# A long-convolution and expert-routing kernel: the first step's frequencies get a DRAM tensor of their own, and the second head's loads and six pieces move behind the first products

## Chip, core and metric

The kernel runs on one core of one Trainium2 chip. The metric is the device time of one execution in microseconds. An execution is taken as the median of several runs.

## What is computed

For each of 4 sequences of 11,456 positions and 128 channels, `u = x * v` is convolved along the sequence with a filter that a small network makes from position embeddings, and the result is multiplied by `x`. Each row then goes, if a skip score is positive, through one of eight experts.

```python
h_filt = (np.maximum(pos_emb @ w1, 0.0) @ w2) * np.exp(-0.01 * pos)[:, None]
u = x * v
Uf = np.fft.rfft(u, n=2 * S, axis=1)
Hf = np.fft.rfft(h_filt, n=2 * S, axis=0)
y = x * np.fft.irfft(Uf * Hf[None, :, :], n=2 * S, axis=1)[:, :S, :]
# then: skip_score = rows @ w_skip; top-1 of 8 experts on the rows with a positive score,
# out = row + gate * relu(row @ w1[e]) @ w2[e]
```

## The kernel before, in words

The transform is done as small matrix products, in blocks of 3,840 positions (60 x 64). The 128 channels are cut into four quarters of 32, which the code calls heads (`NP = 4`, index `h`).

**First phase** (`first_phase`, `First`). Step by step, 16 steps for one head, `load` brings a 768 KB piece of x and v through SyncE's queue (L190, `wf<-xv`, three buffers), `mult` multiplies them (L197), `data` transforms the product on TensorE in two pieces (L214), ScalarE copies them out of PSUM (L216), and `store` writes 720 KB to the DRAM tensor `x1d[h]` through ScalarE's queue (L202, `x1d<-wf`, four buffers). The transform of the filter (`filt`) is woven between; GpSimd's queue stores it in 16 stores of 720 KB to `x1f` (L270).

**Second phase** (`freq_phase`). It takes four of the 60 frequencies at a time: 15 steps for one head, 60 in all; step n is called an iteration here. `load(n)` brings 256 KB of constants (L383, first head only), 768 KB of `x1d[h]` (L386) and 192 KB of `x1f` (L387), all through SyncE's queue, and three iterations ahead. `spread` makes the second transform (L400) with copies by ScalarE (L404); `join` and `mult` on VectorE multiply by the filter (L411 to L420); GpSimd adds the blocks (L493, L494); `back` transforms back on TensorE (L435), and `store` writes z (L447).

The first phase does head 0 alone. The steps of heads 1 to 3 (`others`, a generator) are done inside the second phase as pieces between its products, two pieces for a step, with the multiplication on GpSimd from step 19 on. `step` counts how many pieces are due in an iteration. In head 0 that is two, and four in some iterations. `others` multiplies one step ahead: it calls `mult(n + 1)` before `data(n)`. In the kernel before, the first three steps of head 1 (16 to 18: six pieces, `LEAD`) are done between the first loads and the first products, and the loads of their x and v are issued already in the first phase, since `ahead` looks three steps forward.

Each engine runs its instructions in the order of the program. What sets the order around the change is this order on SyncE's, ScalarE's and GpSimd's queues, and a load of `x1d[0]` waits for all 16 stores to that tensor.

Of the kernel before, what the change touches and what calls it, by code (L numbers as in the profile page):

```python
# [12 lines left out]
F32 = mybir.dt.float32  # L13
# [11 lines left out]
K1, N2 = 60, 64  # L25
L = K1 * N2
H2 = N2 // 2
NS = NB * B
N = L * NS
NP = 4  # L30
DH = D // NP
# [15 lines left out]
LEAD = 6  # L47
FLEAD = 2
FEND = 2
KS = 4  # L50
# [105 lines left out]
class First:  # L156
# [3 lines left out]
    Q = 2  # L160
# [2 lines left out]
    ALL = NP * STEPS  # L163
    XV, US, XS = 3, 2, 4

    def __init__(self, nc, i, x1d, x1f, mc, stage):
        self.nc, self.i, self.x1d, self.x1f = nc, i, x1d, x1f
        n = self.Q * self.RUN
        at = [0]

        def piece(k):
            at[0] += k * n
            return stage[:, at[0] - k * n:at[0]]
        self.xv = [piece(2).rearrange("n (a c) -> n a c", a=2) for _ in range(self.XV)]
        self.us = [piece(1) for _ in range(self.US)]
        self.xs = [piece(2)[0:2 * K1] for _ in range(self.XS)]
        self.used = at[0]
        self.c1 = mc.tile([128, 2 * K1], F32, name="c1")
        nc.sync.dma_start(self.c1, i["c1"])
        self.loaded, self.late = 0, []  # L180

    def ahead(self, step, most=XV):

        while self.loaded < min(step + most, self.ALL):
            self.load(self.loaded)
            self.loaded += 1

# [10 lines left out]

    def store(self):

        for dst, xs in self.late:
            self.nc.scalar.dma_start(dst, xs)  # L202
        self.late = []

    def data(self, step, pool):
        nc, Q, RUN = self.nc, self.Q, self.RUN
        h, ch = divmod(step, self.STEPS)
        u = self.us[step % self.US]
        xs = self.xs[step % self.XS].rearrange("k (m w) -> k m w", w=RUN)
        for q in range(Q):  # L210
            ps = [pool.tile([2 * K1, 512], F32, name="ps")[:, 0:RUN] for _ in range(2)]
            for p in range(2):
                rows = slice(p * 64, p * 64 + K1)
                nc.tensor.matmul(ps[p], self.c1[rows], u[rows, q * RUN:(q + 1) * RUN], start=True, stop=True)  # L214
            for p in range(2):
                nc.scalar.copy(xs[:, 2 * q + p], ps[p])  # L216
            if q < Q - 1:
                yield
        self.late.append((self.x1d[h][:, :, 2 * Q * ch:2 * Q * (ch + 1)].rearrange("k c m w -> (k c) m w"), xs))
        self.store()  # L220
        yield

# [69 lines left out]
def first_phase(tc, fi):  # L292

    with (
        tc.manual_schedule(),
        tc.tile_pool(name="fc", bufs=1) as fc,
        tc.tile_pool(name="fp", bufs=2) as fp,
        tc.tile_pool(name="fps", bufs=4, space=PSUM) as fps,
    ):
        f = fi.filt(fc, fp, fps)  # L300
        left = 0.0
        pieces = NB * 64 * H2 // 512 + 2 * NB * H2 // 4
        pace = (pieces - FLEAD) / (fi.Q * (fi.STEPS - FEND))
        next(f)
        fi.ahead(0, 1)
        next(f)
        fi.ahead(0)
        fi.mult(0)
        for _ in range(FLEAD):
            next(f)  # L310
        for step in range(fi.STEPS):
            for n, _ in enumerate(fi.data(step, fps)):
                if n == 0:
                    fi.ahead(step + 1)
                    if step < fi.STEPS - 1:
                        fi.mult(step + 1)
                left += pace
                while left >= 1:
                    left -= 1
                    next(f, None)  # L320
        for _ in f:
            pass


def freq_phase(tc, nc, i, fi, zd, c3, spare, loads):
# [9 lines left out]
    with (  # L335
# [9 lines left out]
        def c2(k, n=1):  # L345
            t, k = (spare, k) if k < HERE else (rest, k - HERE)
            return t[:, k * 128:(k + n) * 128]
        done = [0]

        def others():  # L350

            fi.mult(fi.STEPS)
            for n in range(fi.STEPS, fi.ALL):
                fi.mult(n + 1)
                fi.ahead(n + 1)
                for _ in fi.data(n, qps):
                    done[0] += 1
                    yield
# [18 lines left out]
        def load(n):  # L377
            h, k = divmod(n, PER)
            while done[0] < h * fi.STEPS * fi.Q:
                next(todo)  # L380
            ks = slice(KS * k, KS * k + KS)
            if h == 0:
                nc.sync.dma_start(c2(ks.start, KS), i["c2"][k])  # L383
            x1 = qx.tile([128, KS, (NS + NB) * DH], F32, name="x1")
            w = NB * DH
            nc.sync.dma_start(x1[:, :, 0:fi.RUN], fi.x1d[h][ks].rearrange("k c n w -> (c n) k w"))  # L386
            nc.sync.dma_start(x1[:, :, fi.RUN:], fi.x1f[ks, :, :, h * w:(h + 1) * w].rearrange("k c n w -> (c n) k w"))  # L387
            return x1

        def spread(n, j):  # L390
# [61 lines left out]
        todo = others()  # L452
        ys = {}
        xs = {n: load(n) for n in range(QX - 1)}
        for _ in range(LEAD):
            next(todo)
        xps, due = {}, []

        def begin(n, j):
            if n < ALL:  # L460
                spread(n, j)
        begin(0, 0)
        begin(0, 1)
        for n in range(ALL + LAG):
            back = backer(n - LAG, ys.pop(n - LAG)) if n >= LAG else lambda lo, hi: None
            if n + QX - 1 < ALL:
                xs[n + QX - 1] = load(n + QX - 1)
            if n >= ALL - PER:
                next(loads, None)

            def half(j):
                join(n, j)
                mult(y, n, j, 0)
                mult(p1, n, j, 1)
                mult(p2, n, j, 2)
                del xps[n, j]
            if n < ALL:
                y = ys[n] = qp.tile([128, NV, 2, NB, B, DH], F32, name="y", bufs=3)
                p1 = qp.tile([128, NV, 2, NB - 1, B, DH], F32, name="p1")
                p2 = qp.tile([128, NV, 2, 1, B, DH], F32, name="p2")  # L480
                half(0)
            step()
            begin(n + 1, 0)
            piece()
            back(0, 2)
            store(nc.sync if n < ALL - 4 else nc.scalar)
            if n < ALL:
                half(1)
                del xs[n]
            begin(n + 1, 1)  # L490
            if n < ALL:
                if n < ALL - 1:
                    nc.gpsimd.tensor_tensor(y[:, :, :, 1:], y[:, :, :, 1:], p1, ALU.add)  # L493
                    nc.gpsimd.tensor_tensor(y[:, :, :, 2:], y[:, :, :, 2:], p2, ALU.add)  # L494
                else:
                    nc.gpsimd.tensor_tensor(y[:, :, :, 1], y[:, :, :, 1], p1[:, :, :, 0], ALU.add)
                    nc.vector.tensor_tensor(y[:, :, :, 2], y[:, :, :, 2], p1[:, :, :, 1], ALU.add)
                    nc.vector.tensor_tensor(y[:, :, :, 2], y[:, :, :, 2], p2[:, :, :, 0], ALU.add)
            piece(ALL)
            back(2, NB)  # L500
        store(nc.scalar)


# [559 lines left out]
def out_phase(tc, i, out, zd, ex, consts):  # L1063
# [6 lines left out]
    with (  # L1070
# [3 lines left out]
      with (  # L1074
# [257 lines left out]
        for q, x in enumerate(ahead):  # L1332
            load(q, x)
# [94 lines left out]
def program(tc, i, out):  # L1428
    nc = tc.nc
    x1d = [nc.dram_tensor(f"x1d{h}", (K1, 2, N2, NS * DH), F32).ap() for h in range(NP)]  # L1430
    x1f = nc.dram_tensor("x1f", (K1, 2, N2, NB * D), F32).ap()
    zd = nc.dram_tensor("zd", (2, NP, H2 * 2 * K1 + ZR, NS * DH), F32).ap()
    lists = nc.dram_tensor("lists", (ROOM // PL, PL), I32).ap()
    with tc.tile_pool(name="mc", bufs=1) as mc:
        wf = mc.tile([128, 2 * E * F], F32, name="wf")
        fi = First(nc, i, x1d, x1f, mc, wf)
        spare = wf[:, fi.used:]
        c3 = mc.tile([128, NV, 128], F32, name="c3")
        first_phase(tc, fi)
        nc.scalar.dma_start(c3, i["c3"])  # L1440
        nc.scalar.dma_start(zd.rearrange("p h r w -> (p h) r w")[:, H2 * 2 * K1:], i["none"])
        later = {}

        def prepare():

            later["ex"] = Experts(tc, i, out, lists, mc, wf)
            yield
            later["consts"] = out_consts(nc, i, mc)
            for e in range(E):
                if e % 2 == 0:  # L1450
                    yield
                later["ex"].weights(e, 0)

            for e in range(E):
                if e != 1:
                    yield
                later["ex"].weights(e, 1)
        freq_phase(tc, nc, i, fi, zd, c3, spare, prepare())
        out_phase(tc, i, out, zd, later["ex"], later["consts"])
# [55 lines left out]
```

## Time and profile before

| | us |
|---|---|
| median of 3 runs | 1555.54 |
| lowest and highest | 1553.31, 1558.93 |
| the profiled execution | 1556.24 |
| its span, first to last instruction | 1554.5 |

The span holds the first phase up to about 125 us, the second phase up to about 690 us, and then the way back and the experts. TensorE is busy for 95% of the span, by the page.

### The profile page before, as it was taken

The numbers are of one execution on the slowest core, as the hardware profiler recorded it, in microseconds if no ns is written. First come the engines' busy times: TensorE is split into PE (matmuls) and PEld (weight loads), VectorE is DVE, ScalarE is ACT, GpSimd is POOL, SyncE is SP. The second block draws the span as 40 slices with busy tenths as digits, with TensorE's granted clock in tenths as the row PEclk, the third lists the DMA queues.
The fourth block names the chain that finished last, engine by engine and source line by source line (L and its number), as shares of the span: only waits on it lengthen the run. The fifth ranks groups of instructions, "written<-read, shape, count | busy, mean of one in ns | idle before, by whom it ended". The sixth has DMA issues, their size and how long they took to land. (4 is left out here: it accounts for less than half of the span.)

```text
span 1554.5 us, 27988 instructions
## 1 busy us (share of the span) xinstructions
PE 1477.4 (95%) x9149; PEld 902.4 (58%) x9149; DVE 1057.0 (68%) x2356; ACT 790.3 (51%) x1643; POOL 965.7 (62%) x808
## 2 busy tenths in 40 slices
PE   7994999999999999979899999999989999999997
PEld 3551344444444434434477666666667788888887
DVE  1322876777777788866876666666658877777773
ACT  4552555555555544433455454454535555556554
POOL 0100876777777766630576459528956888888765
PEclk9997999999999999989899999999999999999999
DMA  9999999999999989989877778778521111111100
GB/s 331 312 334 342 367 385 385 369 370 364 358 384 363 310 252 340 312 291 339 276 260 218 234 229 256 252 216 241 169 57 40 43 46 45 46 46 43 40 29 25
DMA packets 199289, 362.20 MB, mean 233 GB/s; under 512 B 64508, under 2 KB 138762, under 8 KB 199102
## 3 DMA queue, kind: packets, MB, share of 16 engines
q1 hardware_dynamic: 173462, 272.15, 51.9%
q10 hardware_dynamic: 10192, 52.51, 9.1%
q0 software_dynamic: 15488, 35.74, 8.4%
q8 instruction: 74, 1.21, 0.3%
q14 instruction: 73, 0.60, 0.1%
HBM read 216.89 MB, written 145.42 MB: 233 GB/s over the span
## 5 line engine op out<-in xcount | busy, mean ns | idle before, releaser
L746 POOL DMA_INDIRECT out<-o,ids x182 | 197.1, 1083 | 149.0 <-DVE o L753 112.5
L493 POOL TENSOR_TENSOR y<-y,p 128x1536 f32<-128x1536 f32 x59 | 203.6, 3450 | 98.3 <-DVE p L420 98.3
L435 PE MATMUL ps<-y,c 64*128 64x256 f32 (+1 forms) x1440 | 258.9, 490 | 3.5 <-ACT wf L216 2.7
L675 POOL DMA_INDIRECT xt<-out,ids x182 | 192.1, 1056 | 47.9 <-issue 23.5
L435 PEld LDWEIGHTS ps<-y,c 64*128 64x128 f32 x1440 | 138.6, 187 | 116.5 <-issue 83.0
L891 DVE SCALAR_TENSOR_TENSOR hh<-hp,hh 128x1024 fp32r<-128x1024 f32 (+1 forms) x124 | 150.0, 1210 | 79.2 <-ACT hh L890 79.1
L404 ACT COPY xx<-xp 128x480 f32<-128x480 f32 x240 | 112.9, 523 | 127.2 <-PE xp L400 95.1
L438 ACT COPY z<-ps 128x512 f32<-128x512 f32 x240 | 103.6, 482 | 138.3 <-PE ps L435 129.0
L890 ACT ACTIVATE hh<-hp 128x1024 fp32r<-128x1024 f32 (+1 forms) x124 | 127.6, 1029 | 90.0 <-PE hp L742 87.1
L420 DVE TENSOR_TENSOR p<-xp,xx 128x768 f32<-128x768 f32 x240 | 169.4, 748 | 0.0
L420 DVE TENSOR_TENSOR y<-xp,xx 128x1152 f32<-128x1152 f32 x120 | 162.9, 1357 | 4.1
L411 DVE TENSOR_TENSOR xx<-xp,xx 128x384 f32<-128x384 f32 x120 | 66.7, 556 | 127.0 <-ACT xx L404 127.0
L400 PE MATMUL xp<-x,wf 128*64 128x480 f32 x512 | 118.7, 586 | 21.3 <-DMA x<-x1f 17.3
L833 PEld LDWEIGHTS bank<-wd,h 128*128 128x128 f32 x896 | 104.2, 191 | 32.8 <-issue 25.9
L648 POOL MEMSET idle<- 128x512 f16 x226 | 122.4, 542 | 0.3
L216 ACT COPY wf<-ps 120x384 f32<-120x384 f32 x256 | 111.4, 501 | 21.9 <-PE ps L214 12.7
L197 POOL TENSOR_TENSOR wf<-wf 124x768 f32<-124x768 f32 x45 | 81.8, 1818 | 64.2 <-DVE xx L411 35.0
L214 PE MATMUL ps<-wf,c 60*120 60x384 f32 x512 | 118.4, 527 | 2.7 <-ACT wf L216 1.6
L626 POOL DMA_INDIRECT lists<-pl,lies x32 | 51.5, 1609 | 105.5 <-DVE step L1257 52.3
L833 PE MATMUL bank<-wd,h 128*128 128x128 f32 x896 | 114.5, 281 | 1.3 <-DVE o L753 1.3
L494 POOL TENSOR_TENSOR y<-y,p 128x768 f32<-128x768 f32 x59 | 107.2, 1817 | 4.6
L1159 PE MATMUL y<-zt,c 128*64 128x512 f32 x344 | 96.9, 632 | 10.9 <-issue 9.0
(183 smaller groups left out, 2898.7 us busy)
## 6 DMA issues: line engine op xcount, KB each, us to landing
wf<-xv SPq DMA_DIRECT2D x64, 768.0 KB
x1d<-wf ACTq DMA_DIRECT2D x64, 720.0 KB
x<-x1d SPq DMA_DIRECT2D x60, 768.0 KB
zt<-zd SPq DMA_DIRECT2D x58, 768.0 KB
zd<-z SPq DMA_DIRECT2D x108, 384.0 KB
out<-xm SPq DMA_DIRECT2D x96, 258.0 KB
ox<-xo SPq DMA_DIRECT2D x96, 256.0 KB
x1f<-fx POOLq DMA_DIRECT2D x16, 720.0 KB
```

The costliest lines, as they stand in the source:

```text
L214: nc.tensor.matmul(ps[p], self.c1[rows], u[rows, q * RUN:(q + 1) * RUN], start=True, stop=True)
L400: nc.tensor.matmul(xp[p * 64:(p + 1) * 64, c, 0:(NS + NB) * DH], c2(n % PER * KS + k)[:, c * 64:(c + 1) * 64], x1[:, k], start=True, stop= ...
L404: nc.scalar.copy(xx[:, 2 * c, 0:w], xp[:, c, 0:w])
L420: nc.vector.tensor_tensor(o[:, :, j].rearrange("p v m b d -> p v (m b) d"), v[:, :, None, s * DH:(s + 1) * DH].broadcast_to([128, NV, m, DH]),
L435: nc.tensor.matmul(zps[p], c3[r, v], yv[r, v, :, lo:hi], start=(v == 0), stop=(v == NV - 1))
L493: nc.gpsimd.tensor_tensor(y[:, :, :, 1:], y[:, :, :, 1:], p1, ALU.add)
L648: self.nc.gpsimd.memset(self.idle, 0.0)
L675: ins = nc.gpsimd.indirect_dma_start(out=xt[:, j], out_offset=None, in_=self.rows[0:have], in_offset=bass.IndirectOffsetOnAxis(ap=ids[:, j ...
L746: ins = nc.gpsimd.indirect_dma_start(out=self.rows, out_offset=bass.IndirectOffsetOnAxis(ap=ids[:, j:j + 1], axis=0), in_=o, in_offset=Non ...
L833: nc.tensor.matmul(bank[:, j * D:(j + 1) * D], h[f // nf][:, k:k + 128], wd[u][:, f * D:(f + 1) * D], start=(f == 0), stop=(f == F // 128 ...
L890: nc.scalar.activation(v[:, 0], hp, AF.Relu)
L891: nc.vector.scalar_tensor_tensor(v[:, 1], hp, 0.0, v[:, 0].bitcast(F32), ALU.max, ALU.subtract)
```

## The change

A DRAM tensor `x1s` takes the first four frequencies of head 0 (`KS = 4`). Each of the 16 stores of head 0 is cut in two: eight rows go to `x1s` through GpSimd's queue, the other 112 rows to `x1d[0]` through ScalarE's queue as before. The first iteration's loads of `x1s` and `x1f` are issued on GpSimd's queue instead of SyncE's. In the first phase `ahead` stops at the last step of head 0; the loads for steps 16 to 18 are issued when `others` first runs. The six pieces come behind `begin(0, 0)` and `begin(0, 1)`, the products of the first iteration.

```diff
     def ahead(self, step, most=XV):
-        while self.loaded < min(step + most, self.ALL):
+        while self.loaded < min(step + most, self.ALL if step >= self.STEPS else self.STEPS):
@@ data
-        self.late.append((self.x1d[h][:, :, 2 * Q * ch:2 * Q * (ch + 1)].rearrange("k c m w -> (k c) m w"), xs))
+        m = slice(2 * Q * ch, 2 * Q * (ch + 1))
+        k = KS if h == 0 else 0
+        if k:
+            self.late.append((nc.gpsimd, self.x1s[:, :, m].rearrange("k c m w -> (k c) m w"), xs[:2 * k]))
+        self.late.append((nc.scalar, self.x1d[h][k:, :, m].rearrange("k c m w -> (k c) m w"), xs[2 * k:]))
@@ first_phase
-                    fi.ahead(step + 1)
+                    fi.ahead(min(step + 1, fi.STEPS - 1))
@@ others
+            fi.ahead(fi.STEPS)
             fi.mult(fi.STEPS)
@@ load
-            nc.sync.dma_start(x1[:, :, 0:fi.RUN], fi.x1d[h][ks].rearrange("k c n w -> (c n) k w"))
-            nc.sync.dma_start(x1[:, :, fi.RUN:], fi.x1f[ks, :, :, h * w:(h + 1) * w].rearrange("k c n w -> (c n) k w"))
+            eng, src = (nc.gpsimd, fi.x1s) if n == 0 else (nc.sync, fi.x1d[h][ks])
+            eng.dma_start(x1[:, :, 0:fi.RUN], src.rearrange("k c n w -> (c n) k w"))
+            eng.dma_start(x1[:, :, fi.RUN:], fi.x1f[ks, :, :, h * w:(h + 1) * w].rearrange("k c n w -> (c n) k w"))
@@ freq_phase
-        for _ in range(LEAD):
-            next(todo)
         xps, due = {}, []
         begin(0, 0)
         begin(0, 1)
+        for _ in range(LEAD):
+            next(todo)
```

## Rows read from the trace of the kernel before

**Rows 1.** Busy time by stretch: us, each engine's busy us, clock, DMA share, GB/s.

```profile
0.00:100.00 100.00, 89.67 (x581) 47.29 (x583) 26.31 (x34) 48.36 (x98) 6.69 (x16) 1.00 0.93 323
100.00:118.00 18.00, 17.65 (x111) 8.91 (x108) 4.50 (x6) 9.68 (x21) 1.56 (x3) 1.00 0.97 338
118.00:126.00 8.00, 6.32 (x28) 3.47 (x27) 2.87 (x3) 5.47 (x15) 0.52 (x1) 1.00 0.94 373
126.00:136.00 10.00, 1.62 (x8) 0.75 (x8) 0.00 (x0) 2.29 (x6) 0.00 (x0) 0.60 0.93 322
...
150.00:175.00 25.00, 20.46 (x102) 7.94 (x102) 23.08 (x34) 11.92 (x28) 21.15 (x10) 1.00 1.04 388
175.00:180.00 5.00, 5.00 (x32) 2.15 (x28) 3.33 (x6) 2.79 (x7) 3.54 (x2) 1.00 0.94 312
180.00:206.00 26.00, 26.00 (x132) 10.79 (x132) 19.84 (x30) 14.66 (x34) 21.19 (x9) 1.00 1.02 377
206.00:253.00 47.00, 45.91 (x241) 20.72 (x242) 33.51 (x48) 25.81 (x61) 35.45 (x16) 1.00 1.03 386
```

**Rows 2.** SyncE's queue: wait (total, times, longest us), then loads (start, us).

```profile
SPq L386 <- DMA x1d<-wf: 18.3, 2, 15.4
...
132.51 0.39 SPq L386 DMA_DIRECT2D x<-x1d  x1
136.33 0.37 SPq L387 DMA_DIRECT2D x<-x1f  x1
```

**Rows 3.** Timeline of GpSimd (start us, us, what): filter store, iterations with two steps.

```profile
118.01 0.52 POOL L270 DMA_DIRECT2D x1f<-fx  x1 [0.32 <-ACT fx L264]
...
204.27 3.76 POOL L197 TENSOR_TENSOR wf<-wf 124x768 f32<-124x768 f32 x2 [0.47 <-PE ps L214]
207.99 3.43 POOL L493 TENSOR_TENSOR y<-y,p 128x1536 f32<-128x1536 f32 x1
...
255.99 1.81 POOL L197 TENSOR_TENSOR wf<-wf 124x768 f32<-124x768 f32 x1 [0.66 <-DMA wf<-xv]
```

**Rows 4.** Timeline of VectorE and TensorE: step 18's product, first products, first join.

```profile
124.88 0.96 DVE L197 TENSOR_TENSOR wf<-wf 124x768 f32<-124x768 f32 x1 [3.68 <-DMA wf<-xv]
...
144.88 5.17 PE L400 MATMUL xp<-x,wf 128*64 128x480 f32 x16 [17.27 <-DMA x<-x1f]
...
149.36 0.56 DVE L411 TENSOR_TENSOR xx<-xp,xx 128x384 f32<-128x384 f32 x1 [23.52 <-ACT xx L404]
```

**Rows 5.** DMA, 0 to 140 us: GB/s in 40 slices, then issues, KB each.

```profile
GB/s 99 316 410 413 400 214 375 341 424 381 277 191 305 309 292 317 328 346 363 367 321 302 298 248 324 369 390 320 348 303 344 349 365 335 392 355 337 335 293 303
...
wf<-xv SPq DMA_DIRECT2D x19, 768.0 KB
x1d<-wf ACTq DMA_DIRECT2D x19, 720.0 KB
x1f<-fx POOLq DMA_DIRECT2D x16, 720.0 KB
post<-post SPq DMA_DIRECT2D x12, 256.0 KB
```

**Rows 6.** Timeline of ScalarE (start us, us, what): stores of steps 13, 15; a copy.

```profile
114.15 0.32 ACTq L202 DMA_DIRECT2D x1d<-wf  x1
...
121.36 0.32 ACTq L202 DMA_DIRECT2D x1d<-wf  x1
...
125.04 1.63 ACT L216 COPY wf<-ps 120x384 f32<-120x384 f32 x4 [1.63 <-DMA x1d<-wf]
```

**Rows 7.** The page's groups: GpSimd's indirect loads, busy us and mean ns.

```profile
L675 POOL DMA_INDIRECT xt<-out,ids x182 | 192.1, 1056 | 47.9 <-issue 23.5
```

**Rows 8.** DMA, 140 to 270 us: GB/s in 40 slices of 3.25 us.

```profile
GB/s 359 217 379 411 395 375 369 383 394 380 402 287 308 415 344 329 425 394 392 382 394 393 380 406 348 357 395 364 411 406 384 398 387 376 408 411 395 393 384 296
```

**Rows 9.** One stretch as in rows 1, and TensorE's timeline in it.

```profile
255.00:260.00 5.00, 3.39 (x15) 2.29 (x16) 2.16 (x3) 2.11 (x6) 4.34 (x3) 0.76 1.03 399
...
256.88 2.97 PE L435 MATMUL ps<-y,c 64*128 64x256 f32 x12 [1.61 <-ACT wf L216]
```

More of the change, by code (lines that the diff above doesn't have):

```diff
@@ L164, with __init__ @@
     XV, US, XS = 3, 2, 4
-    def __init__(self, nc, i, x1d, x1f, mc, stage):
-        self.nc, self.i, self.x1d, self.x1f = nc, i, x1d, x1f
+    def __init__(self, nc, i, x1s, x1d, x1f, mc, stage):
+        self.nc, self.i, self.x1s, self.x1d, self.x1f = nc, i, x1s, x1d, x1f
         n = self.Q * self.RUN
@@ L199, in store @@
     def store(self):
-        for dst, xs in self.late:
-            self.nc.scalar.dma_start(dst, xs)
+        for eng, dst, xs in self.late:
+            eng.dma_start(dst, xs)
         self.late = []
@@ L1430, in program @@
     x1d = [nc.dram_tensor(f"x1d{h}", (K1, 2, N2, NS * DH), F32).ap() for h in range(NP)]
+    x1s = nc.dram_tensor("x1s", (KS, 2, N2, NS * DH), F32).ap()
     x1f = nc.dram_tensor("x1f", (K1, 2, N2, NB * D), F32).ap()
@@ L1435, in program @@
         wf = mc.tile([128, 2 * E * F], F32, name="wf")
-        fi = First(nc, i, x1d, x1f, mc, wf)
+        fi = First(nc, i, x1s, x1d, x1f, mc, wf)
         spare = wf[:, fi.used:]
```

## The prediction

> **What bounds the kernel now.** I read the table by stretch first: around the change it shows TensorE doing 1.62 us of work in the ten microseconds from 126 [rows 1]. The timelines say why. The first load of the second phase waits 15.4 us for the stores to `x1d` and goes out at 132.51; its `x1f` half goes out at 136.33 [rows 2], when the last filter store, issued at 118.01 [rows 3], has landed. The first products start at 144.88 and the first `join` at 149.36 [rows 4]. That gap is what the change can shorten.
>
> The same table has a second reading, and I think it decides. The DMA engines show a share of 0.93 to 0.97 up to 136 and of 1.02 to 1.04 at 377 to 388 GB/s from 150 to 253, but for a dip to 312 at 175 to 180 [rows 1]. So transfers, and not TensorE alone, pace head 0. Where it hurts is seen on GpSimd in the iterations with two steps: the pair of multiplications at 204.27 takes 3.76 us, 0.14 more than two of 1.81, and the second one of the pair at 255.99 waits 0.66 us for its load of x and v [rows 3]. Slack there is nil: GpSimd's block sums (L493) are queued right behind the pair, at 207.99, and TensorE's way back waits for them.
>
> **What moves ahead of the first load.** Up to 140 us 19 loads of xv, 19 stores to `x1d`, 16 to `x1f` and 12 loads of positions are issued [rows 5]: 14.94 + 14.01 + 11.80 + 3.15 = 43.9 MB, with some 1.0 MB of constants 44.9 MB. The rates add up to 32.3 + 6.1 + 3.0 + 3.2 = 44.6 MB by 136 [rows 1]: the gate at 136.33 is the moment when everything ahead has gone through. The change takes 3 x 768 KB of loads and 3 x 720 KB of stores out of that, 4.57 MB, and leaves 40.3. These bytes were through by 118 + (40.3 - 38.4) / 0.373 = 123. But step 15's stores are issued only at 121.36 [rows 6], by the engines' pace; one takes between 2.0 us (720 KB at 373 GB/s) and the 10.9 us from 114.15 to 125.04 of step 13's [rows 6]. With the queues nearly empty I take 4: the gate falls at 125.5 instead of 136.3, between 123 and 130.
>
> **The own tensor and GpSimd's queue.** Sixteen more stores at 0.52 us [rows 3] are 8.3 us on GpSimd, which is all but idle there (1.56 us of 18, 0.52 of 8) [rows 1]. The two loads cost GpSimd between 0.52 us each and, by rows handled, 8 x 1.06 = 8.4 us for both (1,024 short rows against 128 of an indirect load [rows 7]); I take the lower end, the direct transfer being nearest. The new wait on GpSimd holds up the `x1f` half, the first multiplications of `others` and the first block sums; all need later data. The load of `x1s` cannot bring the first products forward alone, because they need `x1f` too, gated 3.8 us later than `x1d` before.
>
> **First products.** From the gate to the first product it took 144.88 - 136.33 = 8.6 us: now 125.5 + 8.6 = 134, plus 5.2 for the sixteen products [rows 4], 139.3. With the high GpSimd price 142 and 147.
>
> **The six pieces.** Their loads now stand on SyncE's queue behind the loads of iterations 1 and 2, and VectorE's three multiplications (0.96 us each [rows 4]) stand ahead of the first `join`. So the join waits for step 18's load: three iterations' x1 (2.95 MB), constants 0.26 and xv 2.36, 5.6 MB, behind a start-up of about 2 us (the kernel's first 3.5 us slice moved 99 GB/s against 316 in the next [rows 5]). At 322 to 388 GB/s that is 14 to 17 us: 142 to 145, and with the last multiplication the join at 143 to 146; I take 145, at most 148 with the gate late, against 149.36. Behind those loads on SyncE wait the xv of steps 19 to 21 (each for its buffer) and the fourth iteration's loads, which so shift with the join. The engines are 4.4 us ahead here. Counted alone that is 1556.24 - 4.4 = 1551.8.
>
> **What takes it back.** The six transfers are not gone, only later, and the DMA engines stand still meanwhile. At 125.5 before had moved 41.2 MB, after 40.3: 0.9 behind. Start-up of 2 us at 345 GB/s: another 0.7. The dip at 175 to 180 gives back (388 - 312) x 5 us = 0.38 MB, since the engines now feed the queues earlier; so does the slice of 3.25 us from 143 on at 217 GB/s between 359 and 379 ([rows 8], the second slice), some 0.45 MB, a pause that comes from SyncE's short queue at that point. That leaves 0.8 MB, at 385 GB/s 2.1 us. Up to 206 both kernels need the same bytes, so the pair's second multiplication, at 206.2 before, comes at about 208: the 4.4 us become a wait of 6.5 us on GpSimd, then on TensorE. The pair at 256 meets full queues again (1.03 [rows 1]), so the delay stays. From there on all is shifted alike. The sum: 1556.24 + 2.1 = 1558.3 for the profiled execution, and 0.7 less against the median of 1555.54: **1557.6**. With the gate 2.5 us either way and start-up between 0 and 4 us: 1553.5 to 1561.
>
> In the ten microseconds from 126, when little but ScalarE's stores is under way, 322 GB/s are moved, and 388 from 150 on [rows 1]; no row shows single engines. [...]
>
> **Rivals.** (1) The start is kept, faster: the loads of the pairs are late by their place in the queue, not for want of bandwidth, and come earlier with everything else. For it: the dip at 175 to 180, and slack before the ordinary iterations. Against it: shares over 1.0 everywhere else and bytes that do not shrink. Then 1555.5 - 4.4 = 1551.1, and with the join at its earliest, 142.5, 1548.7. [...] (3) The change does not do what it says: the last `x1f` store, still in GpSimd's queue with the small stores, lands as late as before (136), because its share of the DMA engines does not grow when the other two queues fall idle. Then first products at 145, six pieces behind them, the join at some 152, 2.6 later than before, and by the pair most of that is covered by the loads: 1558.
>
> **How the numbers follow.** A measurement of this kernel can tell some 0.3% from no change, 4.7 us: below 1550.9 and above 1560.2. Forecast 0.60, of which 0.06 lies above; rival 1 0.20, of which 0.13 below 1550.9; rival 2 0.12, 0.10 above; rival 3 0.08, 0.01 above. Faster 0.13, same 0.70, slower 0.17. Range 1550.5 to 1562: it leaves out the far ends of rivals 1 and 2.
>
> **What would show it.** Right: GpSimd's loads of `x1s` and `x1f` issued at about 126, first products near 134, the first join near 145, a DMA rate well under 338 GB/s somewhere between 110 and 128, and GpSimd's first pair of multiplications in one iteration split, its second half waiting for xv until about 208. Wrong: a pair without a wait while the join is early (rival 1), or a low granted clock after both pairs with loads long there (rival 2), or loads on GpSimd at 134 or later (rival 3). The forecast falls if DMA engines in 150 to 206 move clearly more than 390 GB/s.

## The result and the profile after

| | before | after |
|---|---|---|
| median | 1556.44 (5 runs) | 1568.33 (5 runs) |
| lowest, highest | 1553.31, 1558.93 | 1561.16, 1570.41 |
| profiled execution, its span | 1556.24, 1554.5 | 1561.16, 1559.4 |

The changed kernel is slower: ratio 1.0065, 95% interval 1.0040 to 1.0089 (the two medians alone give 1.0076). The forecast was 1557.6 us, range 1550.5 to 1562. The profiled execution is the fastest of its five, so its trace shows the smaller part of the loss, 4.9 us.

The table by stretch, as in [rows 1] (us, each engine's busy us, clock, DMA share, GB/s):

```profile
0.00:100.00 100.00, 84.70 (x538) 44.09 (x540) 24.75 (x32) 46.14 (x93) 11.32 (x25) 0.97 0.91 314
100.00:118.00 18.00, 18.00 (x138) 10.29 (x136) 6.05 (x8) 9.20 (x20) 3.61 (x7) 1.00 0.89 299
118.00:126.00 8.00, 5.47 (x26) 2.64 (x22) 0.00 (x0) 5.31 (x12) 2.07 (x4) 1.00 0.88 259
126.00:136.00 10.00, 0.00 (x0) 0.00 (x0) 0.00 (x0) 0.00 (x0) 0.94 (x2) 0.62 0.61 184
...
180.00:206.00 26.00, 25.90 (x138) 11.78 (x136) 19.78 (x28) 14.20 (x34) 18.81 (x10) 1.00 1.04 398
```

Two things differ. In the first 100 us TensorE has worked 4.97 us less than before (84.70 against 89.67). And between 126 and 136 us no engine computes at all, while the DMA engines move 184 GB/s at a share of 0.61, against 322 at 0.93. They had room, and the first load waited all the same. The timeline (start us, us, what) shows for how long:

```profile
124.65 0.31 ACTq L202 DMA_DIRECT2D x1d<-wf  x1
124.91 0.52 POOL L202 DMA_DIRECT2D x1s<-wf  x1 [1.58 <-ACT wf L216]
135.06 0.81 POOL L392 DMA_DIRECT2D x<-x1s  x1 [9.63 <-DMA x1s<-wf]
135.37 0.39 SPq L392 DMA_DIRECT2D x<-x1d  x1
135.86 0.78 POOL L393 DMA_DIRECT2D x<-x1f  x1
...
143.76 5.95 PE L406 MATMUL xp<-x,wf 128*64 128x480 f32 x16 [20.27 <-DMA x<-x1f]
...
153.58 0.96 DVE L197 TENSOR_TENSOR wf<-wf 124x768 f32<-124x768 f32 x1 [0.49 <-DMA wf<-xv]
154.45 0.55 DVE L417 TENSOR_TENSOR xx<-xp,xx 128x384 f32<-128x384 f32 x1
```

Step 15's stores are issued at 124.65 and 124.91 us, against 121.36 for the one store of before [rows 6]. The load that waits for the 48 KB of `x1s` goes out 10.15 us later, at 135.06 where 125.5 was forecast, and 0.3 us before the one that waits for the 672 KB of `x1d`. The first products start at 143.76, 1.1 us ahead of [rows 4], but the first join at 154.45, 5.1 us behind it, because the products of steps 16 to 18 now stand in front of it and wait for loads issued after the gate. GpSimd's block sums begin 5.5 us later than before (162.70 against 157.20), the seventh stands 7.6 us later (215.56 against [rows 3]) and the fourteenth 7.1 us (287.75 against 280.69).

Most of that loss falls in four short stretches of the first phase, 65 to 85 us (2.8 of the 4.97 us; 36 of the 43 matmuls that TensorE is behind by at 100 us):

```profile
65.00:70.00 5.00, 1.16 (x4) 0.48 (x4) 1.12 (x2) 1.24 (x3) 0.00 (x0) 0.69 0.99 365
70.00:75.00 5.00, 5.00 (x24) 2.20 (x22) 0.00 (x0) 2.14 (x5) 0.51 (x1) 0.62 0.78 284
75.00:80.00 5.00, 5.00 (x40) 2.82 (x38) 1.46 (x3) 1.84 (x4) 0.54 (x2) 1.00 0.05 21
80.00:85.00 5.00, 5.00 (x40) 2.74 (x38) 1.48 (x2) 2.79 (x6) 1.02 (x2) 1.00 1.03 257
```

and in ScalarE's and TensorE's rows at its start (start us, us, what):

```profile
68.76 0.59 ACT L268 COPY fx<-ps 120x512 f32<-120x512 f32 x1 [4.86 <-DMA x1f<-fx]
69.40 2.91 PE L266 MATMUL ps<-hw,cf 64*120 64x512 f32 x5 [3.84 <-ACT fx L268]
```

ScalarE's waits of that kind in the first 130 us (total, times, longest us):

```profile
ACT fx L268 <- DMA x1f<-fx: 8.1, 2, 4.9
```

ScalarE waits 4.86 us until a store to `x1f` has landed (issued at 51.37; the trace's semaphore events have 16 updates for this store, called its marks here, the first 4.0 us after the issue and the last 17.3, 0.07 us before the copy) and its buffer `fx` is free; TensorE, whose results ScalarE takes out, stops. While nothing new is made, the queues run dry, and between 75 and 80 us the DMA engines move 21 GB/s. And TensorE comes back at a granted clock of 0.62 to 0.69 (means over five microseconds; it is 0.50 from 66.9 to 73.8 us). In the kernel before, ScalarE's waits of that kind and the same four stretches are:

```profile
ACT fx L264 <- DMA x1f<-fx: 7.0, 4, 2.7
...
65.00:70.00 5.00, 3.96 (x28) 2.01 (x26) 1.56 (x2) 1.89 (x4) 0.00 (x0) 1.00 0.96 350
70.00:75.00 5.00, 5.00 (x34) 2.51 (x30) 0.69 (x1) 2.29 (x5) 0.00 (x0) 1.00 0.93 335
75.00:80.00 5.00, 5.00 (x46) 3.38 (x46) 2.09 (x3) 3.26 (x8) 1.03 (x2) 1.00 0.83 274
80.00:85.00 5.00, 5.00 (x36) 2.97 (x34) 1.71 (x3) 2.00 (x5) 0.00 (x0) 1.00 0.94 269
```

The sums of the waits differ by 1.1 us only; what is new is that 4.9 us came in one piece.

### The profile page after: what moved, and what is told of

The parts are those of the page before. It is cut to its first block, busy times and chain, and to the rows that moved or that the text cites. A ratio compares the mean times of both kernels' runs of the same rounds, so it can differ in the third digit from the quotient of the medians.

```text
span 1559.4 us, 28025 instructions
## 1 busy us (share of the span) xinstructions
PE 1475.7 (95%) x9149; PEld 901.8 (58%) x9149; DVE 1056.2 (68%) x2356; ACT 789.7 (51%) x1643; POOL 973.4 (62%) x826
```

## Experiments

Each kernel was timed beside runs of the kernel before on the same chip, and only ratios are compared: between chips the median of before went from 1556 to 1580 us. "Gate" is the time of the first iteration's load of `x1s`, or of `x1d` where there is no `x1s`. f1_split8 and f2_split60 stand below. Each row is one profiled execution, beside a ratio from several. e9_order_fx3 and f4_order_fx3 are the same kernel: their gates lie 3.8 us apart and their first joins 4.7, so a difference of that size between two rows shows nothing by itself.

| kernel | step 15's store issued | gate | first products | first join | ratio, 95% interval |
|---|---|---|---|---|---|
| before | 121.36 | 132.51 | 144.88 | 149.36 | |
| r_before | 122.45 | 134.43 | 145.00 | 149.24 | |
| after | 124.65 | 135.06 | 143.76 | 154.45 | 1.0065, 1.0040 to 1.0089 |
| r_after | 130.94 | 141.11 | 149.89 | 160.54 | 1.0044, 1.0021 to 1.0067 |
| e1_order | 120.92 | 129.56 | 134.91 | 148.79 | 1.0019, 0.9983 to 1.0056 |
| e2_own | 131.96 | 143.76 | 156.04 | 160.52 | 1.0027, 0.9999 to 1.0056 |
| e3_act | 126.70 | 132.54 | 138.67 | 151.60 | 0.9989, 0.9960 to 1.0019 |
| e4_held | 122.59 (x1s) | 128.54 | 134.88 | 162.96 | |
| e5_xvahead | 123.16 | 135.74 | 141.05 | 148.37 | 1.0008, 0.9980 to 1.0036 |
| e6_behind | 125.80 | 134.29 | 139.65 | 144.13 | 1.0095, 1.0061 to 1.0129 |
| e7_fx3 | 117.54 | 134.49 | 144.57 | 152.87 | 1.0021, 1.0002 to 1.0040 |
| e8_before_fx3 | 118.09 | 132.18 | 143.05 | 147.53 | 0.9992, 0.9971 to 1.0013 |
| e9_order_fx3 | 118.67 | 130.62 | 136.00 | 150.78 | 0.9977, 0.9953 to 1.0001 |
| f4_order_fx3 | 118.22 | 126.84 | 132.19 | 146.07 | 0.9982, 0.9965 to 0.9999 |
| f3_whole | 124.17 | 141.73 | 151.30 | 159.35 | 1.0065, 1.0043 to 1.0088 |
| e10_act_fx3 | 123.34 | 130.47 | 137.96 | 149.20 | 1.0009, 0.9992 to 1.0027 |

### The two halves of the change

e1_order keeps the order and drops the tensor; e2_own keeps the tensor and drops the order:

```diff
# e1_order, against the kernel before
-                    fi.ahead(step + 1)
+                    fi.ahead(min(step + 1, fi.STEPS - 1))
# and the limit in ahead(), fi.ahead(fi.STEPS) first in others(), and
-        for _ in range(LEAD):
-            next(todo)
         ...
         begin(0, 1)
+        for _ in range(LEAD):
+            next(todo)
# e2_own: the rest of the change, x1s with its stores and loads on GpSimd's queue
```

> Only the order of the change: the three loads of xv and the six pieces go behind the first products; no tensor x1s, GpSimd's queue as in the kernel before. Theory A (the sixteen stores to x1s on GpSimd's queue slow the first phase and land late): without them the last x1f store is issued at about 118 us as before (after: 121.3), ScalarE's x1d store of step 15 at about 121 (after: 124.7) and lands some 10 us later, the first load of x1d goes out at about 131, the first products at about 140, the join at about 151; time near that of the kernel before plus 2, within 0.3% of it. Theory B (the order alone makes the loss): the join at 154 as in after, time 1.0065 of before. Theory C (the gate falls early once the six pieces are behind it): first load of x1d at about 126.

> Only the tensor of its own: x1s and its loads and stores on GpSimd's queue, xv 16 to 18 and the six pieces ahead of the first products as in the kernel before. Theory A (the stores on GpSimd's queue slow the first phase): step 15's store to x1d is issued at about 125 us, 3 us later than before (121.4); load of x1s at 136 or later, the first join 3 to 4 us later than before's 149.4, time 1.002 to 1.004 of before. Theory B (the order alone makes the loss): step 15's store at 121.4, the join at 149 or earlier, time 1.000 or less.

In e1_order (start us, us, what) the gate falls at 129.56 and the first products start 10.0 us before those of [rows 4]:

```profile
129.56 0.39 SPq L387 DMA_DIRECT2D x<-x1d  x1
...
134.91 6.10 PE L401 MATMUL xp<-x,wf 128*64 128x480 f32 x16 [15.14 <-DMA x<-x1f]
...
143.85 0.96 DVE L197 TENSOR_TENSOR wf<-wf 124x768 f32<-124x768 f32 x1 [29.69 <-DMA wf<-xv]
...
208.52 1.82 POOL L197 TENSOR_TENSOR wf<-wf 124x768 f32<-124x768 f32 x1 [0.21 <-DMA wf<-xv]
```

So the order alone does what the tensor was to do. Of the 10.0 us 0.6 are left at the join (148.79), for VectorE waits for the moved loads of x and v until 143.85. GpSimd's first block sums come 1.7 us earlier than before, the fifth 1.7 us later (191.11 against 189.38) and the seventh, behind the pair of multiplications, 2.3 us later (210.29 against 207.99). Theory A holds for its first phase, theory B falls. e2_own shows the other half: step 15's store at 131.96, 10.6 us later than before, TensorE busy for 14.28 us of 60 to 80, the join 11.2 us late. That was in the direction of theory A and three times its size; in that execution, 8.0 us longer than the median of its kernel, ScalarE waited 13.0 us for stores to `x1f`. Its ratio, 1.0027, lies where theory A had it, but its interval reaches below 1.

### The same kernels a second time

> The changed kernel once more, beside the other variants and the kernel before on one chip. If its loss is the sum of the two parts (tensor and queue, order), it has a ratio of about 1.0046 to 1.0065 here too; if the small stores on GpSimd's queue cost what the start of the second phase showed, its profile has again TensorE at 16 to 17 us busy between 60 and 80 us, the load of x1s at about 135 and the first join at about 154.

> The kernel before, for a second profile: the start of the second phase is set by stores and loads alone and should repeat: first load of x1d at 132 to 133, of x1f at 136, first products at 145, the first join at 149, each within 1 us. If they stray by 3 us or more from one execution to the next, differences of that size between the variants' profiles prove nothing.

The kernel before repeats: first products at 145.00 and first join at 149.24, each within 0.2 us, though its first load goes out 1.9 us later. Its fourteenth block sum does not (276.68 against 280.69), so differences of 4 us that arise after 200 us prove nothing. The changed kernel's ratio, 1.0044, is near the sum of the two halves (1.0019 and 1.0027). Its start does not repeat: the stall comes 4.5 us later and costs more, the stretches of 65 to 85 us again:

```profile
65.00:70.00 5.00, 4.67 (x38) 2.55 (x36) 2.02 (x3) 1.34 (x3) 0.84 (x2) 1.00 0.98 354
70.00:75.00 5.00, 1.08 (x4) 0.56 (x6) 0.23 (x1) 1.35 (x3) 0.08 (x1) 0.81 0.95 351
75.00:80.00 5.00, 5.00 (x20) 2.32 (x18) 0.00 (x0) 2.03 (x4) 0.43 (x1) 0.50 0.65 235
80.00:85.00 5.00, 5.00 (x28) 2.38 (x26) 0.69 (x1) 0.92 (x2) 0.00 (x0) 0.66 0.01 2
```

TensorE's granted clock is 0.50 for a whole stretch, the DMA engines then move 2 GB/s, and step 15's store is issued at 130.94, 6.3 us later than in the first profile. The join follows at 160.54.

### Why the small store lands late

e4_held holds ScalarE's two last stores to `x1d` back until behind the first products; GpSimd's stores to `x1s` and their load stay as they are.

```diff
+        (self.held if self.STEPS - 2 <= step < self.STEPS else self.late).append(last)
         ...
+        fi.late, fi.held = fi.held, []      # behind begin(0, 1); the loads 1 and 2 follow
+        fi.store()
```

> The changed kernel, but ScalarE's stores to x1d of steps 14 and 15 (672 KB each) are held back until behind the first products; the loads of iterations 1 and 2 follow them. Theory L1 (the small store to x1s of step 15, issued on another queue, is not told landed before ScalarE's store of the same step, issued at the same time, has landed): the load of x1s goes out at about 129 us, soon after the x1f stores are through, instead of 135; first products at about 138. Theory L2 (it is late by itself, as any transfer of GpSimd's queue issued behind the x1f stores): still about 135 and 144. The time of the whole is of no use here, since iterations 1 and 2 are loaded later.

GpSimd's rows (start us, us, what):

```profile
122.59 0.52 POOL L202 DMA_DIRECT2D x1s<-wf  x1 [1.03 <-ACT wf L216]
128.54 0.81 POOL L393 DMA_DIRECT2D x<-x1s  x1 [5.42 <-DMA x1s<-wf]
```

5.95 us from store to load, where after has 10.15 and r_after 9.9 (131.20 to 141.11). So the large stores on ScalarE's queue hold the small one up, as theory L1 had it; whether they delay its being told or only share the DMA engines with it, this run does not tell, since it takes 1.4 MB out of the way. Nor does after: its small store has its last mark at 134.47, its large one at 135.17, and the two loads go out at 135.06 and 135.37.

Nor is the queue the small store's own: GpSimd's queue carries the stores to `x1f` too, and theory L2 has its part. In e7_fx3 and f3_whole, further down, the load behind `x1d` goes out at 131.78 and 137.94, and the load of `x1s` only at 134.49 and 141.73, 0.8 us after the load behind `x1f` (133.65 and 140.88). There the small store came with the large ones of its own queue.

### Which queue, and the buffers of the filter

e3_act issues the small stores on ScalarE's queue. e7_fx3 to e9_order_fx3 give the filter's frequencies a third buffer, in the changed kernel, the kernel before and e1_order; e10_act_fx3 does both.

```diff
-            self.late.append((nc.gpsimd, self.x1s[...], xs[:2 * k]))
+            self.late.append((nc.scalar, self.x1s[...], xs[:2 * k]))          # e3_act, e10_act_fx3
-            ... name=f"fx{p}") for p in range(2)]
+            ... name=f"fx{p}", bufs=3) for p in range(2)]                     # e7 to e10, f1 to f4
```

> The changed kernel with its stores to x1s issued by ScalarE, next to those to x1d, instead of by GpSimd; GpSimd still issues the two first loads. Theory A1 (GpSimd's queue, shared by the stores to x1s and x1f, is what slows the first phase): the waits of ScalarE's copies for the landing of x1f stores go from 8.1 back to about 7.0 us, the last x1f store is issued at 118, step 15's store at 122. Theory A2 (the sixteen further small stores cost the DMA engines wherever they are queued): still 121 and 125. In both the load of x1s waits until about 10 us after step 15's store, 132 or 135; time 1.003 or 1.0065 of before.

> The changed kernel with three buffers instead of two for each filter block's frequencies (fx0, fx1). Theory S (the loss is one long stall of the first phase: ScalarE's copies into fx wait 4.9 us in one piece for a store to x1f, TensorE stops, its granted clock falls to 0.5 to 0.7, and the loads run dry, DMA share 0.05 between 75 and 80 us): without the wait TensorE is busy 19 to 20 us of 60 to 80, DMA share above 0.8 in 75 to 85, step 15's store to x1d at about 120 instead of 124.7 to 130.9, the load of x1s at about 130, the first join at about 149; time 0.998 to 1.001 of before instead of 1.0044. Theory Q (GpSimd's queue or the further stores cost by themselves): TensorE's work in 60 to 80 us may fill, but step 15's store stays at 125 or later, time 1.003 or more.

> The kernel before with three buffers for fx0 and fx1. By theory S its shorter waits for stores to x1f (7.0 us, four times, longest 2.7) go too; step 15's store at 119 instead of 121.4. But its first load waits for the transfers ahead of it, which are the same: the first load of x1d at 131 to 132, first products at 143 to 145, time 0.998 to 1.000 of before.

> The order of the change without its tensor, with three buffers for fx0 and fx1. By theory S step 15's store at about 119, the first load of x1d at about 128, the first products at 133, the join at about 147, 2 us before the kernel before. If the DMA engines pace head 0 after that, the second pair of multiplications on GpSimd (about 260 us) is still 0 to 4 us later than before, time 0.999 to 1.002 of before; if the start is kept, 0.998.

> The changed kernel with three fx buffers and its small stores issued by ScalarE (e7_fx3 but for that queue). If GpSimd's queue is what costs: the stores to x1f land within 16 us as in the kernels without x1s, not after 20 to 25; the load of x1s goes out at 130 to 133 instead of 134.5, time 0.997 to 0.999 of before. If the split itself costs, as its lower rate per busy share would have it: load at 134 or later, time 1.001 to 1.003 of before.

e3_act (the stretch of 60 to 80 us, ScalarE's waits for `x1f`, then start us, us, what):

```profile
60.00:80.00 20.00, 20.00 (x152) 11.13 (x148) 6.74 (x9) 9.83 (x22) 2.07 (x4) 1.00 0.97 326
...
ACT fx L268 <- DMA x1f<-fx: 3.1, 2, 2.0
...
126.12 0.55 ACTq L202 DMA_DIRECT2D x1s<-wf  x1
126.70 1.65 ACTq L202 DMA_DIRECT2D x1d<-wf  x1
```

TensorE works through all of 60 to 80 us (after has 16.16 there, r_after 15.75), and the ratio is 0.9989 against r_after's 1.0044, on two chips where the kernel before took 1580.17 and 1580.74 us. The intervals miss each other by 0.0002 (1.0019 and 1.0021); the first measurement's begins at 1.0040. That is the one single edit of the changed kernel that takes the loss away, though not as expected: step 15's store is issued at 126.70, nearer to theory A2's 125 than to A1's 122, because the doubled stores now hold ScalarE (1.98 us for an issue instead of 0.31). But the load of `x1s` goes out 6.4 us after its store instead of 10.

e7_fx3: the stall is gone, and the phase ends early, with step 15's stores at 117.54 and 117.80. The same stretches:

```profile
65.00:70.00 5.00, 5.00 (x48) 3.23 (x46) 1.56 (x2) 3.09 (x8) 0.51 (x1) 1.00 0.98 354
70.00:75.00 5.00, 5.00 (x36) 2.80 (x36) 1.79 (x3) 1.97 (x6) 0.87 (x2) 1.00 0.95 300
75.00:80.00 5.00, 5.00 (x42) 2.89 (x40) 1.15 (x2) 3.06 (x7) 0.69 (x2) 1.00 1.02 299
```

The ratio falls to 1.0021, between theory S (0.998 to 1.001) and theory Q (1.003 or more): theory S holds for the first phase. The gate it missed by 4.5 us. The engines were 7 us earlier, the gate only 0.6. GpSimd's rows (start us, us, what) show the length of the wait:

```profile
117.80 0.52 POOL L202 DMA_DIRECT2D x1s<-wf  x1 [1.58 <-ACT wf L216]
134.49 0.81 POOL L392 DMA_DIRECT2D x<-x1s  x1 [16.17 <-DMA x1s<-wf]
```

and so does the rate of the DMA engines in 40 slices of 0.625 us from 112 to 137:

```profile
GB/s 285 315 334 256 324 315 275 295 315 275 315 295 305 275 256 324 305 285 305 246 246 256 157 236 197 157 118 108 79 49 59 39 20 71 125 369 398 377 123 294
```

Up to 125 us the queues are full, and then the rate sinks from 236 to 20 GB/s in six microseconds before the gate opens. f4_order_fx3 and e9_order_fx3, one kernel with the same three buffers and without `x1s`, in the same view:

```profile
GB/s 393 403 383 285 236 246 226 167 256 334 383 315 275 324 315 305 315 334 266 275 265 187 69 0 0 96 91 354 401 377 338 342 380 369 378 324 313 358 378 371
...
GB/s 334 393 413 256 256 88 216 256 216 285 334 364 295 246 344 295 305 315 285 305 305 275 118 69 49 29 39 39 29 0 0 84 71 356 403 381 339 326 345 347
```

In f4_order_fx3 the rate breaks off within 2 us, and SyncE's first load goes out at 126.84. In e9_order_fx3 it trickles on at 29 to 118 GB/s for some 4 us, and the load goes out at 130.62. So such a tail is no mark of `x1s`.

What does part the kernels is how long the stores to `x1f` take. By the semaphore events of the trace, those issued from 40 to 100 us (us from issue to the last mark):

| | mean | slowest |
|---|---|---|
| two buffers, `x1s` on GpSimd's queue (after, r_after, e2_own, e4_held) | 12.4 to 13.0 | 16.5 to 19.3 |
| two buffers, e3_act and five profiles without `x1s` | 10.5 to 11.5 | 14.7 to 17.3 |
| three buffers, `x1s` on GpSimd's queue (e7_fx3, f3_whole) | 15.7, 16.4 | 25.0, 26.5 |
| three buffers, e10_act_fx3 and five profiles without `x1s` | 12.2 to 13.4 | 16.2 to 20.6 |

That is the link between the small stores and ScalarE's waits: on GpSimd's queue they make the stores to `x1f` slower, on ScalarE's they do not.

e10_act_fx3 gave the gate that its queue theory named (130.47); its slowest store to `x1f` took 20.6 us, not 16, and its time, 1.0009, lies between the two theories. Its interval overlaps e7_fx3's, so with three buffers the times do not part the two queues. e8_before_fx3 came out as expected, no faster than before. e9_order_fx3 was 2.6 us later than expected at its gate and 3.8 at its join, and its twelfth block sum (261.84) 4.1 us later than before, yet its ratio, 0.9977, is what the theory of a kept start had named.

### What the split costs the DMA engines

The share of DMA time and the rate from 40 to 118 us, one divided by the other, part the kernels: 339 to 348 GB/s for a full share where head 0's stores are whole (before 324 / 0.94 = 345, e8_before_fx3 331 / 0.95 = 348, e6_behind 298 / 0.88 = 339), 321 to 333 where 8 rows are split off (after 295 / 0.89 = 331, e3_act 308 / 0.94 = 328, e7_fx3 308 / 0.96 = 321). Three kernels, all with three `fx` buffers, take that apart, and a fourth repeats e9_order_fx3:

```diff
# f1_split8: 8 and 112 rows into x1d, both by ScalarE; f2_split60: 60 and 60
-        self.late.append((self.x1d[h][...], xs))
+        for r in (slice(0, 8), slice(8, 2 * K1)) if h == 0 else (slice(0, 2 * K1),):
+            self.late.append((x[r], xs[r]))
# f3_whole, against e7_fx3: x1d takes all 120 rows again, x1s its 8 besides
-        self.late.append((nc.scalar, self.x1d[h][k:, :, m]..., xs[2 * k:]))
+        self.late.append((nc.scalar, self.x1d[h][:, :, m]..., xs))
```

> The order of the change with three fx buffers (as e9_order_fx3), each store to x1d of head 0 in two: 8 rows and 112 rows, both by ScalarE, into x1d itself; no tensor x1s, nothing on GpSimd's queue but x1f. Theory W (splitting 120 rows into 8 and 112 makes the DMA engines move less): 40 to 118 us at about 325 GB/s per busy share (the changed kernel 331, e7_fx3 321), as against 345 of e9_order_fx3; last store issued at 118 to 122, first load of x1d 2 to 4 us later than its 130.6. Theory Q (it takes GpSimd's queue or a tensor of its own): 345 and 130 to 131.

> The same with 60 and 60 rows. If it is the number of stores that costs, about 325 GB/s per busy share here too; if it is the 8 and 112 rows, 345, with the first load of x1d at 130 to 131.

> The changed kernel with three fx buffers (as e7_fx3), but ScalarE's store to x1d takes all 120 rows again, and GpSimd stores the 8 rows to x1s besides (48 KB twice, 0.8 MB more in all). If the 112 rows are what costs: 345 GB/s per busy share, the load of x1s at 130 to 132 instead of 134.5, time 0.997 to 0.999 of before instead of 1.0021. If the small store costs: still about 325, the load at 134 or later, time 1.002 or more.

> The order of the change with three fx buffers once more (as e9_order_fx3, 0.9977 of before, 0.9953 to 1.0001). If that was more than scatter, 0.996 to 0.999 here, with an interval below 1 when both are taken together; if not, 0.999 to 1.002.

f1_split8 has 306 / 0.93 = 329 and its gate at 133.04, f2_split60 293 / 0.92 = 318 and 139.64, f3_whole 317 / 0.92 = 345. So with the 120 rows cut in two the DMA engines move fewer bytes per busy share, whichever queue and tensor, and 60 and 60 rows are no better than 8 and 112; the further small store as such does not do it, since f3_whole has that too. (The gates of f1_split8 and f2_split60 lie 2.4 and 9.0 us behind that of e9_order_fx3; the first is within what one kernel shows.) But f3_whole, with the rate restored, has the longest time of the kernels with three buffers: 1.0065. There a store to `x1f` issued at 120.81 holds its load until 140.88, the `x1s` store of 124.43 holds its own until 141.73, and ScalarE waits 4.2 us for `x1f` in spite of three buffers. The rate per share is therefore not what decided. What f3_whole shares with e7_fx3 and the changed kernel is the small stores on GpSimd's queue, and its stores to `x1f` are the slowest of all (26.5 us).

f4_order_fx3 repeats e9_order_fx3 at 0.9982, 0.9965 to 0.9999: with a third buffer the order alone is the one version that came out ahead of both kernels, by some 3 us. How much of that is the order and how much the third buffer is open, since the interval of e8_before_fx3 (0.9971 to 1.0013) overlaps.

### The pieces' place

e5_xvahead moves only the pieces and leaves their loads in the first phase. e6_behind takes e1_order and puts the six pieces behind iteration 0.

```diff
# e6_behind, against e1_order
-        for _ in range(LEAD):
-            next(todo)
         for n in range(ALL + LAG):
             ...
             begin(n + 1, 1)
+            if n == 0:
+                for _ in range(LEAD):
+                    next(todo)
```

> The order of the change without its tensor, and the six pieces and their loads of xv one place later: behind the whole of iteration 0's join and multiplications instead of between its products and its join. Both theories: first load of x1d at about 130, first products at 135, the first join at about 140 instead of 149. Theory D (the DMA engines pace head 0, so a start that comes earlier turns into waits for the loads): GpSimd's first block sums come 8 us earlier than before, and by the iterations with two steps (about 200 us) no more than 2 us of it is left; time 0.999 to 1.002 of before. Theory E (the start is kept): still 7 us or more at 260 us, time 0.995 to 0.996 of before.

> The kernel before with one edit: the six pieces behind the first products; their three loads of xv stay in the first phase. Theory F (of the two moves the pieces' stores are what held the first load back): the stores of steps 16 to 18 no longer stand ahead of it, first load of x1d at about 130, first products at 138 to 140 (the three loads of xv, 2.3 MB or 6 us, still stand ahead of the loads of x1), the first join at 143 to 146, earlier than with the loads moved too (148.8), since its multiplications need not wait. Theory G (the loads of xv ahead are what held it back): first load at 132, products at 144. By theory D of another run (the DMA engines pace head 0) the time is within 0.2% of before in both.

e5_xvahead: neither F nor G for the gate. Step 15's store needs 12.6 us to land behind 2.3 MB of further loads, the gate is at 135.74, and what the join wins by having its x and v at hand it loses there: 148.37 against e1_order's 148.79. Its time is that of before, as both theories had it. e6_behind has the shortest way from gate to join (9.8 us), and is the slowest of all. It missed both theories:

```profile
144.13 0.56 DVE L412 TENSOR_TENSOR xx<-xp,xx 128x384 f32<-128x384 f32 x1 [25.09 <-ACT xx L405]
...
152.88 0.96 DVE L197 TENSOR_TENSOR wf<-wf 124x768 f32<-124x768 f32 x1 [5.17 <-DMA wf<-xv]
```

The loads of x and v now stand behind those of a fourth iteration, VectorE waits 5.17 us for the first of them with everything of iteration 1 queued behind, and GpSimd's first block sums come at 169.91, 12.7 us later than before. It does not decide between D and E, since its start was never ahead at the sums. (Its first phase also had a stall like that of after, TensorE 17.57 us busy in 60 to 80, without `x1s`: two buffers can stall in any of these kernels. All four profiles with `x1s` on GpSimd's queue and two buffers had one, of the other six, e3_act among them, this one alone.)

## Why the prediction was wrong, point by point

- **The gate: wrong, and the step that failed.** It was put at 125.5 and measured 135.06 and 141.11. Two terms of it were mis-sized. Step 15's store was taken at 121.36, "by the engines' pace"; it was issued at 124.65 and 130.94, since the pace of the first phase hung on stores to `x1f`, which the change put in one queue with sixteen small ones. And the landing was taken as 4 us from a range of 2.0 to 10.9 "with the queues nearly empty"; it was 10.15 and 9.9. This term fails without the small stores too: in e1_order, f4_order_fx3 and e9_order_fx3 the load goes out 8.6, 8.6 and 12.0 us after step 15's store. The engines were at a share of 0.61, but by the semaphore events the 672 KB of step 15 in after gave their first mark 6.3 us after the issue and their sixteenth after 10.5, at 135.17, and the load that waited for them went out at 135.37. The prediction's rows held longer landings than its range: 121.36 to 132.51, 11.2 us, for step 15's own store, and 118.01 to 136.33, 18.3 us, for the filter's. So the gate at 136.33 was not "the moment when everything ahead has gone through" but the landing of one slow store; by the semaphore events the store of step 18 landed at 142.4.
- **GpSimd's price: half right.** The stores cost GpSimd 0.51 to 0.52 us each and the loads 0.81 and 0.78, near the low end that was taken. The cost lay not on the engine but on its queue, and no term of the sum had weighed that: e3_act, with the queue changed and nothing else, has 0.9989.
- **From gate to products: right in number, in part by luck.** 8.6 us forecast; 135.06 to 143.76 is 8.7. The 8.6 were carried over from a start with the transfers of steps 16 to 18 under way. With these moved and the first load on SyncE's queue it is 5.4 in e1_order, f4_order_fx3 and e9_order_fx3; in the kernels that load on GpSimd's queue it is 6.1 to 12.3.
- **From gate to join: right.** 125.5 to 145 is 19.5; measured are 135.06 to 154.45, 19.4. The join behind the six pieces waits for the loads of steps 16 to 18, as told.
- **What takes it back: right in kind, smaller, and not at the pair.** 6.5 us were to be lost between the join and the first pair, as one wait of the pair's second multiplication at about 208. In e1_order it stands at 208.52, but behind a wait of 0.21 us (0.83 in after): the lead had gone before, most of it by the fifth block sum. Of e1_order's lead 4.0 us go between the first and the seventh block sum (1.7 ahead, then 2.3 behind), of f4_order_fx3's 3.8 (152.74 and 207.31 against 157.20 and 207.99). In after there was no lead to take, and 2.1 us were lost on top.
- **Rival 1, start kept:** no. There was no earlier start in after, and where there was (e1_order, f4_order_fx3) most of it went.
- **Rival 2, TensorE's clock:** the granted clock fell to 0.50 at 66.9 to 73.8 us, far ahead of the pairs; after the second pair it is 0.86 over 260 to 272 us (0.96 in before), and from the seventh sum on nothing more is lost, as far as one profile tells. No run shows a cost of the clock at the pairs, the term behind the upper end of the range, 1562.
- **Rival 3, the change does not do what it says:** its sign came true (loads on GpSimd at 134 or later, join 152 or later), not its reason and not its price. The last `x1f` store landed before the rest (at 132.0, by the semaphore events), and the loads did not cover the late join: 1558 forecast, 1568.33 measured. It was given 8 in 100.
- **The split stores themselves:** the sum has no term for what a store of 112 rows takes against one of 120. By the semaphore events, of the 16 marks of a whole store of 120 rows one comes at its issue (0.5 us in most) and 15 from 3.4 us on (before), of a store of 112 rows all 16 come from 3.0 us on (after). Nothing was gained by it: the split stores go at 331 GB/s per full share instead of 345, and at 318 for 60 and 60 rows.

Of the 11.9 us between the medians, the first profile accounts for 4.9 and the second shows that the same stall can cost 6.3 more; that the slower executions of after all had the larger stall is argued, not shown, as each gave no trace. That the small stores on GpSimd's queue are the cause of the stall rests on e3_act and on the landings of the stores to `x1f` (on average 12.4 us in both profiles of after and 10.5 in e3_act, 15.7 in e7_fx3 and 13.0 in e10_act_fx3). Why they slow that queue is open, and with three buffers the times alone do not show it.

## What to carry to other kernels

Here a load's gate was the last mark of the slowest store that it waited for (before: 132.37, and the load at 132.51; after: 135.17 and 135.37), and on GpSimd's queue, which carried large stores too, a small store did not come clearly ahead of the large ones issued with it (in e7_fx3 its load went out 0.8 us after the load behind `x1f`): take the longest landing that the trace shows, not bytes over rate. Before stores are added to a queue, ask which buffer of another loop is released by that queue, because a wait of 4.86 us there came back as DMA engines at 21 GB/s and a granted TensorE clock of 0.50. An earlier start is worth measuring for itself (moving the pieces and their loads gave 10 us at the first products), and then what stands next in line decides how much of it arrives.

## What the runs showed of the hardware

- A stall of 4.86 us was followed by five microseconds at 21 GB/s (r_after: 2 GB/s), and TensorE's granted clock was 0.50 from 66.9 to 73.8 us (r_after: in the stretch of 75 to 80 us). The sixteen first products, behind gaps of 13.2 to 28.3 us, took 4.83 to 6.21 us.
- With a store of 120 rows cut in two the DMA engines moved 318 to 333 GB/s for a full share, without the cut 339 to 348, in 9 profiles against 9.
- Issues by ScalarE mostly took 0.31 us, and two together as much as 3.12 us (f1_split8) and 4.71 us (f2_split60) where its stores are doubled.
- 48 KB stores on GpSimd's queue between stores of 720 KB made these land later: 12.4 to 13.0 us on average against 10.5 to 11.5, and with three buffers 15.7 and 16.4 against 12.2 to 13.4.
